# Output products of small experts as full-precision half-array matmuls, in a three-layer kernel on one core

## The chip, the cores and the metric

The kernel runs on one core of a Trainium2 chip. The core has a matrix engine (TensorE, PE in the rows; its weight loads are listed as PEld), a vector engine (VectorE, DVE), a scalar engine (ScalarE, ACT), GpSimd (POOL) and SyncE (SP), which issues most of the transfers. They share one on-chip memory (SBUF) and the accumulators of TensorE (PSUM, eight banks). The metric is the device time of one execution in microseconds (us), the median of several runs.

## The reference

Three layers follow one another: a retention with a decaying state, a dense feed-forward layer, and a routed layer of eight experts.

```
# 1: batch 2, heads 8, 768 steps, head size 64
state = gamma * state + k_t (outer) v_t ;  y_t = scale * q_t @ state
# 2: 1536 tokens, 512 -> 2048 -> 512
h = x @ w_in ;  x = max(0.01 h, h) @ w_out
# 3: each token goes to its best expert e, at most 384 tokens each
e = argmax(x @ w_gate) ;  gate = softmax(x @ w_gate)[e]
out = gate * (max(x @ w1[e], 0) @ w2[e])      # 512 -> 1024 -> 512
```

With the inputs of the reference the router sends 144, 395, 35, 77, 80, 27, 183 and 595 tokens to experts 0 to 7. Of expert 7, 384 are kept, and 128 of these are computed in a pass of their own ahead of the expert loop, so that 256 are left for its body.

## The kernel before

**Precision.** Where a product has to be precise, an operand is split into a high part of reduced precision (`hi`, `gh`) and the rest (`lo`, `gl`), and three one-pass products stand for one: `PROD`, L350, is hi·hi, hi·lo, lo·hi. A plain full-precision (f32) matmul needs no splits; in the trace it shows as two matmul records, each with its own weight load. The split of a weight tile is `conv` (L855): ScalarE writes `hi`, VectorE then writes `lo`.

**The front.** Up to L1040 the program zeroes a tile, runs nine 128x512 matmuls on zeros (L1034), clears one bank (L215) and starts the loads. Then a list written out by hand (`FRONT`, L40) sets the order of the retention and of the first units of the dense layer. After its first entry, the scores `S.0`, stand 22 small matmuls on zeros (L1086). The loop from L1131 on runs the rest of the dense layer; for its first 24 units it also writes three one-element ScalarE instructions each (`tick`, L1155).

**The experts.** `expert(s, cls, o)` (L903) is one expert's body for `cls` tiles of 128 tokens. All three sizes are in the program, and branches on the token count (L1250, L1251) choose one at run time, on each engine by itself. `name_next` (L982) places a hint on the coming branch. A body has eight units `u` of 128 hidden columns. For each, `mm_h` (L825) makes the hidden values, `ew_h` (L876) applies the relu and splits, and `mm_y` (L883) adds the unit to the output bank `yps`. With one tile, `mm_h` takes the f32 weights as they landed (`raw(u)`), four f32 matmuls of 128 columns, and all eight units' hidden values come before the first `mm_y` (`LAGS[1]` is 8). `mm_y` always takes the splits, three matmuls of 512 columns per unit. At unit 6 (one tile) the next expert's rows are transposed (`prep_x`, L779), and the gather of the rows after those is issued.

**Weights.** A unit's weights are one transfer of 512 KB. They land in 15 buffers (`LAND + XLAND`), so that `refill` (L895, issued on SP) of the buffer of unit u loads unit u+15. It waits until u's buffer has been read for the last time. The splits have 8 buffers (`RING + XRING`); `conv_next` (L913) converts the rest of the body's units and the first three of the next body, and may go no further than 8 units past the last `mm_y` (`read`).

**The end of a body.** `evac` (L989) scales the bank by the gate on ScalarE, and `scatter` (L995) writes the rows out with an indirect transfer.

Of the kernel before, what the change touches and what calls it, by code (L numbers as in the profile page):

```python
# [14 lines left out]
ACTF = mybir.ActivationFunctionType  # L15
ALU = mybir.AluOpType
# [43 lines left out]
def retention_moe_moe_kernel(ctx: ExitStack, tc: tile.TileContext, qkv, wb, wc, wg, const, out, cap):  # L60
# [279 lines left out]
    def counts(s):  # L340
        return [r[s // slabs] for r in regs]
# [507 lines left out]
    def raw(u):  # L849
        return craw[slot_of(u, LAND + XLAND)]  # L850
# [21 lines left out]
    def g_of(u, cls):  # L872
        i = u // 4 % 2 if cls == 1 else 0
        return [x[:, i * P:(i + cls) * P] for x in gpair[u % 4]]

    def ew_h(u, cls):  # L876
        hp = h_of(u, cls)
        gh, gl = g_of(u, cls)
        nc.scalar.activation(out=gh, in_=hp, func=ACTF.Relu)  # L879
        nc.vector.scalar_tensor_tensor(out=gl, in0=hp, scalar=0.0, in1=gh.bitcast(F32),  # L880
                                       op0=ALU.max, op1=ALU.subtract)

# [20 lines left out]
    def expert(s, cls, o):  # L903
        u0 = s * PF
        lag = LAGS[cls]
        last = s + 1 == NS
        todo = [(u, cls) for u in range(u0 + (2 if s == 0 else 3), u0 + PF)]
        todo += [(u, 2) for u in range(u0 + PF, min(NU, u0 + PF + 3))]
        filled = [u0]

        read = [u0]

        def conv_next():  # L913
            if todo and todo[0][0] < read[0] + RING + XRING:
                conv(*todo.pop(0))

        def hidden(k):
            u = u0 + k
            r = mm_h(u, cls)
            if u == HOLD or s and k == 0 and cls > 1:  # L920
                held[0] = r
            yield
            ew_h(u, cls)
            conv_next()

        def refills(k):
            if s == 0 and k < HOLD:
                return
            top = todo[0][0] if todo else u0 + PF
            while filled[0] < min(top, u0 + k + 1, u0 + PF):  # L930
                refill(filled[0] + LAND + XLAND)
                filled[0] += 1

        if s == 0:
            finish_all(prep_x(0, cls))
            if NS > 1:
                load_x(1)
            pre_end()
            conv_next()
        xg = None  # L940
        for i in range(lag + PF):
            if i == NAME[cls] and not last:
                name_next(s + 1)
            if i == PREP[cls] and not last:
                xg = prep_x(s + 1)
                step(xg)
                if s + 2 < NS:
                    load_x(s + 2)
            h = hidden(i) if i < PF else None
            if h:  # L950
                step(h)
            k = i - lag
            if k >= 0 and not (last and k >= PF - 2):
                mm_y(u0 + k, cls, range(cls))
                read[0] = u0 + k + 1
            if h:
                step(h)
            else:
                conv_next()
            if i == PREP[cls] and xg is not None:  # L960
                finish_all(xg)
            refills(i)
        while todo:
            conv_next()
        refills(PF)
        for t in range(cls):
            if last:
                for v in (u0 + PF - 2, u0 + PF - 1):
                    mm_y(v, cls, [t])
            evac(s, o, t)  # L970
            scatter(s, o, t)

    def load_counts():
# [15 lines left out]
    def evac(s, o, t):  # L989
        if t == 1:  # L990
            nc.vector.tensor_scalar(out=o[t], in0=yps[t], scalar1=gate(s, t), scalar2=None, op0=ALU.mult)
        else:
            nc.scalar.activation(out=o[t], in_=yps[t], func=ACTF.Copy, scale=gate(s, t))
# [32 lines left out]
    with tc.manual_schedule():  # L1026
# [4 lines left out]
        nc.scalar.activation(out=bias_e, in_=zero[:, 0:1], func=ACTF.Copy)  # L1031
        tick = sm_p.tile([1, 1], F32, name="tick", bufs=1)
        wm = bank("y2", [P, DM])
        for i in range(9):  # L1034
            nc.tensor.matmul(out=wm, lhsT=zb[:, 0:P], rhs=zb[:, 0:DM], start=True, stop=True)
        zero_state(0)
        first_const.append(lambda: load_const(C_D, C_D + 1024))
# [39 lines left out]
        for n in names:  # L1077
            n, c = n.split(".")
            c = [int(x, 16) for x in c]
            if n == "ev" and not rows_l:  # L1080
                early.close()
                rows_p = right.enter_context(tc.tile_pool(name="rows", bufs=1, side="right"))
                rows_l.append(rows_p.tile([P, NT, DM], F32, name="rows"))
            parts[n](*c)
            if n == "S" and c[0] == 0:
                for _ in range(22):  # L1086
                    nc.tensor.matmul(out=wm[0:32, 0:64], lhsT=zb[:, 0:32], rhs=zb[:, 0:64], start=True, stop=True)
            reached += n == "H"
            key = {"S": "q", "qs": "q", "M": "k", "D": "k", "ks": "k"}.get(n)
            if key:  # L1090
                users[key, c[0]].discard(n)
                if not users[key, c[0]]:
                    used((key, c[0]))
# [37 lines left out]
        for i in range(reached, len(units)):  # L1131
# [18 lines left out]
            slot()  # L1150
            if i == len(units) - 1:
                break
            if i - reached < 24:
                for _ in range(3):
                    nc.scalar.activation(out=tick, in_=zero[0:1, 0:1], func=ACTF.Copy)  # L1155
            u = units[i - LAG]
# [169 lines left out]
```

## Time and profile before

| | before |
|---|---|
| median of 3 runs | 524.3 us (523.18, 524.3, 525.4) |
| the profiled execution, its own time | 523.39 us |
| its span, first to last instruction | 521.6 us |
| outside the span | 1.79 us |
| TensorE busy | 506.6 us, 97% of the span |
| VectorE, ScalarE busy | 65%, 49% |
| mean granted TensorE clock | 0.992 |

The busy shares come from one profiled execution. A matmul's duration overlaps the next one's, so that the pace of a row of matmuls is read from the distance between starts. In the trace the bodies of experts 0 to 7 begin on TensorE at 353, 380, 415, 428, 441, 455, 468 and 491 us; experts 2 to 5 take the body for one tile. Where TensorE waits is read from the idle time ahead of its instructions; where its clock falls, from the granted clock of a short stretch.

### The profile page before, as it was taken

Reading aid. Unit: us, or ns where it says so; the run is one execution under the profiler, and the core shown is the slowest. Engines: PE = TensorE matmul, PEld = TensorE weight load, DVE = VectorE, ACT = ScalarE, POOL = GpSimd, SP = SyncE. Lnnn points to the kernel's source line nnn. Section 1 sums busy time; section 2 is a strip of 40 time slices with the busy share of each in tenths; the row PEclk is TensorE's granted clock in tenths of the full one; section 3 lists DMA queues with packets and bytes.
Section 4 is the critical chain, followed back from the end, with each engine's and each line's share of the span. In section 5 each row is a group of like instructions: output and inputs, shape, how many; then the busy total and the mean of one; then the engine's idle time right before and its main releaser. Section 6 shows DMA issues by size and latency. Waiting matters only on the chain.

```text
span 521.6 us, 9204 instructions
## 1 busy us (share of the span) xinstructions
PE 506.6 (97%) x3421; PEld 453.8 (87%) x3421; DVE 337.6 (65%) x666; ACT 253.4 (49%) x573; POOL 49.6 (10%) x79
## 2 busy tenths in 40 slices
PE   7899999999999999999999999999989999999994
PEld 5888989999999999999998888789789899899893
DVE  3999994279779847974732545767544366676550
ACT  2886964365545534442423314346433466666340
POOL 0000000000000000000100106344000121210101
PEclk9999999999999999999999999999989999999998
DMA  8977672022315712220201107589354099992001
GB/s 312 396 261 272 225 252 101 1 81 82 102 31 147 238 50 75 87 80 1 80 1 62 61 1 266 205 283 328 143 198 166 24 369 347 358 351 79 33 1 46
DMA packets 24941, 80.81 MB, mean 155 GB/s; under 512 B 3706, under 2 KB 3834, under 8 KB 24864
## 3 DMA queue, kind: packets, MB, share of 16 engines
q1 hardware_dynamic: 21312, 70.26, 38.6%
q0 software_dynamic: 3552, 9.58, 5.1%
q8 instruction: 41, 0.67, 0.5%
q14 instruction: 36, 0.29, 0.2%
HBM read 72.35 MB, written 9.96 MB: 158 GB/s over the span
## 4 chain that ended last, share of the span: by engine, by line
PE 72%; DMA 22%; DVE 2%; issue 1%; ACT 1%; POOL 0%; SPq 0%; POOLq 0%; ACTq 0%; DVEq 0%
PE ps_h L363 25%; PE ps_y L414 16%; DMA out<-og,gix 12%; PE ps_a L414 7%; DMA xr<-x2d,gix 7%; PE ps_h L837 5%; PE ps_y L889 5%; PE ps_a L190 2%; PE ps_a L256 2%; PE ps_a L245 2%; PE ps_h L715 1%; DMA xpre<-wc,wix 1%; DMA cst<-cst_in 1%; PE ps_y L726 1%; PE ps_h L228 1%
## 5 line engine op out<-in xcount | busy, mean ns | idle before, releaser
L370 ACT ACTIVATE hs<-ps_h 128x384 f32<-128x384 f32 x64 | 31.4, 490 | 95.9 <-PE ps_h L363 95.9
L375 DVE SCALAR_TENSOR_TENSOR hs<-hs 128x384 f32<-128x384 f32 x64 | 35.6, 556 | 65.3 <-ACT hs L370 65.1
L414 PE MATMUL ps_y<-hi,gh 128*128 128x512 f32 x138 | 56.4, 409 | 0.0
L363 PE MATMUL ps_h<-xh,hi 128*128 128x384 f32 x256 | 56.3, 341 | 0.0
L363 PE MATMUL ps_h<-xl,hi 128*128 128x384 f32 x256 | 55.5, 338 | 0.0
L363 PE MATMUL ps_h<-xh,lo 128*128 128x384 f32 x256 | 55.5, 338 | 0.0
L379 ACT ACTIVATE gh<-hs 128x384 fp32r<-128x384 f32 x64 | 33.7, 526 | 43.8 <-DVE hs L375 43.8
L414 PE MATMUL ps_y<-hi,gl 128*128 128x512 f32 x138 | 53.9, 391 | 0.0
L414 PE MATMUL ps_y<-lo,gh 128*128 128x512 f32 x138 | 53.8, 390 | 0.0
L363 PEld LDWEIGHTS ps_h<-xh,hi 128*128 128x128 f32 x256 | 45.9, 188 | 4.8
L385 DVE TENSOR_TENSOR gl<-hs,gh 128x384 fp32r<-128x384 f32 x64 | 35.6, 557 | 21.3 <-ACT gh L379 21.3
L363 PEld LDWEIGHTS ps_h<-xl,hi 128*128 128x128 f32 x256 | 45.9, 187 | 0.0
L363 PEld LDWEIGHTS ps_h<-xh,lo 128*128 128x128 f32 x256 | 45.8, 187 | 0.0
L889 PE MATMUL ps_y<-hi,gh 128*128 128x512 f32 x104 | 41.1, 395 | 0.0
L889 PE MATMUL ps_y<-hi,gl 128*128 128x512 f32 x104 | 40.8, 392 | 0.0
L889 PE MATMUL ps_y<-lo,gh 128*128 128x512 f32 x104 | 40.8, 392 | 0.0
L860 DVE TENSOR_TENSOR lo<-xland,hi 128x1024 fp32r<-128x1024 f32 (+1 forms) x32 | 33.5, 1056 | 7.2 <-ACT hi L859 7.1
L880 DVE SCALAR_TENSOR_TENSOR gl<-ps_h,gh 128x256 fp32r<-128x256 f32 (+2 forms) x42 | 16.6, 395 | 33.1 <-ACT gh L879 30.4
L879 ACT ACTIVATE gh<-ps_h 128x256 fp32r<-128x256 f32 (+2 forms) x42 | 15.3, 364 | 39.6 <-PE ps_h L837 22.9
L860 DVE TENSOR_TENSOR lo<-land,hi 128x1024 fp32r<-128x1024 f32 (+1 forms) x30 | 30.9, 1042 | 5.4 <-ACT hi L859 5.4
L414 PEld LDWEIGHTS ps_y<-hi,gl 128*128 128x128 f32 x138 | 25.9, 188 | 5.6
L414 PEld LDWEIGHTS ps_y<-hi,gh 128*128 128x128 f32 x138 | 25.9, 187 | 4.3 <-issue 0.3
(201 smaller groups left out, 998.1 us busy)
## 6 DMA issues: line engine op xcount, KB each, us to landing
land<-wc SPq DMA_DIRECT2D x32, 512.0 KB, 6.6
xland<-wc SPq DMA_DIRECT2D x32, 512.0 KB, 5.9
land<-wb SPq DMA_DIRECT2D x31, 512.0 KB, 4.9
land<-qkv SPq DMA_DIRECT2D x19, 512.0 KB, 5.3
out<-zero SPq DMA_DIRECT2D x12, 256.0 KB, 5.7
x2d<-rows SPq DMA_DIRECT2D x12, 256.0 KB, 2.2
early<-qkv SPq DMA_DIRECT2D x5, 512.0 KB, 7.4
cst<-cst_in SPq DMA_DIRECT2D x1, 512.0 KB, 5.5
```

Of the source, the lines that this page charges most:

```text
L190: nc.tensor.matmul(out=at["s", c][h2][:, a, :], lhsT=kT[r, a, :], rhs=qT[r, a, :], start=True, stop=True)
L363: nc.tensor.matmul(out=h_ps, lhsT=w[i][:, dc * P:(dc + 1) * P], rhs=x[j][:, dc, :], start=(n == 0), stop=(n == 3 * KD - 1))
L370: nc.scalar.activation(out=hs, in_=gt[u][0], func=ACTF.Copy)
L375: nc.vector.scalar_tensor_tensor(out=hs, in0=hs, scalar=0.01, in1=hs, op0=ALU.mult, op1=ALU.max)
L379: nc.scalar.activation(out=gh, in_=gt[u][0], func=ACTF.Copy)
L385: nc.vector.tensor_tensor(out=gl, in0=hs, in1=gh.bitcast(F32), op=ALU.subtract)
L414: nc.tensor.matmul(out=yb[ti][t], lhsT=gt[u][i][:, t * P:(t + 1) * P], rhs=w[j][:, 512:1024], start=(f == fs[0] and n == 0), stop=(f == fs ...
L837: r = nc.tensor.matmul(out=hp, lhsT=w[i][:, dc * P:(dc + 1) * P], rhs=(h, l)[j][:, dc, 0:cls * P], start=(n == 0), stop=(n == 3 * KD - 1))
L860: nc.vector.tensor_tensor(out=lo[:, o], in0=src[:, o], in1=hi[:, o].bitcast(F32), op=ALU.subtract)
L879: nc.scalar.activation(out=gh, in_=hp, func=ACTF.Relu)
L880: nc.vector.scalar_tensor_tensor(out=gl, in0=hp, scalar=0.0, in1=gh.bitcast(F32), op0=ALU.max, op1=ALU.subtract)
L889: nc.tensor.matmul(out=yps[t], lhsT=gg[i][:, t * P:(t + 1) * P], rhs=w[j][:, 512:1024], start=(k == 0 and n == 0), stop=(k == PF - 1 and n ...
```

## The change

- **`ew_h`:** with one tile, ScalarE also writes an f32 copy of the relu of the first 64 tokens (`g_half`, 64 columns per unit, in the no longer needed mask part of `cst`).
- **`y_group` in place of `mm_y`, one-tile bodies only:** the output products stand in two groups of four units, each with a branch on TensorE. With at most 64 tokens a unit is one f32 matmul of 64 by 512, straight on `raw(u)`; even units write partitions 0 to 63 of the bank, odd units 64 to 127. Otherwise the group is the old split products.
- **`join`:** with at most 64 tokens, ScalarE copies the upper half of the bank to SBUF and VectorE adds it, times the gate, to the output rows. Both have a branch of their own.
- **`refills`:** in one-tile bodies a buffer may be refilled only after its `y_group` (`read`), since that group may read it.
- **The start:** 27 small and 5 wide matmuls on zeros instead of 9 wide ones; the 22 small ones after `S.0` go; the `tick` instructions stop after 11 units, not 24.

The conversions of all weights stay, also those that a body with at most 64 tokens does not read.

```diff
+    def g_half(u):
+        return cst[:, C_D + u % PF * 64:C_D + u % PF * 64 + 64]
+    def few(s, cls):
+        return (s % slabs) * BW + cls * P - 64
+    def y_group(s, cls, ks):
+        us = [s * PF + k for k in ks]
+        t = cls - 1
+        with tc.If(counts(s)[0] <= few(s, cls)) as c:
+            for u in us:
+                k = u % PF
+                nc.tensor.matmul(out=yps[t][k % 2 * 64:k % 2 * 64 + 64, :], lhsT=g_half(u), rhs=raw(u)[:, 512:1024],
+                                 start=(k < 2), stop=(k >= PF - 2), skip_group_check=True)
+        with c.Else():
+            for u in us:
+                mm_y(u, cls, [t])
+    def join(s, cls, o):
+        part = cst[0:64, C_D + 512:C_D + 1024]
+        with tc.If(counts(s)[1] <= few(s, cls)):
+            nc.scalar.activation(out=part, in_=yps[cls - 1][64:P, :], func=ACTF.Copy)
+        with tc.If(counts(s)[2] <= few(s, cls)):
+            nc.vector.scalar_tensor_tensor(out=o[0:64, :], in0=part, scalar=gate(s, cls - 1)[0:64, :],
+                                           in1=o[0:64, :], op0=ALU.mult, op1=ALU.add)
 def ew_h(u, cls):
         nc.scalar.activation(out=gh, in_=hp, func=ACTF.Relu)
+        if cls == 1:
+            nc.scalar.activation(out=g_half(u), in_=hp[:, 0:64], func=ACTF.Relu)
 def expert(s, cls, o):
-            while filled[0] < min(top, u0 + k + 1, u0 + PF):
+            while filled[0] < min(top, u0 + k + 1, u0 + PF, read[0] if cls == 1 else NU):
...
-            if k >= 0 and not (last and k >= PF - 2):
+            if cls > 1 and k >= 0 and not (last and k >= PF - 2):
                 mm_y(u0 + k, cls, range(cls))
                 read[0] = u0 + k + 1
+            if cls == 1 and k in (0, 4):
+                end = PF - 2 if last and k else k + 4
+                y_group(s, cls, range(k, end))
+                read[0] = u0 + end
...
             evac(s, o, t)
+            if cls == 1:
+                join(s, cls, o[t])
             scatter(s, o, t)
 the start
-        for i in range(9):
+        for i in range(27):
+            nc.tensor.matmul(out=wm[0:32, 0:64], lhsT=zb[:, 0:32], rhs=zb[:, 0:64], start=True, stop=True)
+        for i in range(5):
             nc.tensor.matmul(out=wm, lhsT=zb[:, 0:P], rhs=zb[:, 0:DM], start=True, stop=True)
...
-            if n == "S" and c[0] == 0:
-                for _ in range(22):
-                    nc.tensor.matmul(out=wm[0:32, 0:64], lhsT=zb[:, 0:32], rhs=zb[:, 0:64], start=True, stop=True)
...
-            if i - reached < 24:
+            if i - reached < 11:
                 for _ in range(3):
                     nc.scalar.activation(out=tick, in_=zero[0:1, 0:1], func=ACTF.Copy)
```

The order of the instructions, at three places. First TensorE in the one-tile body of expert 2, where the hidden products (L831) end and the output products begin (before):

```order
L831 MATMUL ps_y<-cxf,xland 128x128 x5
L758 UNCONDITIONAL_BRANCH x2
L831 MATMUL ps_y<-cxf,xland 128x128 x3
L889 MATMUL ps_y<-hi,gh 128x512
L889 MATMUL ps_y<-lo,gh 128x512
L889 MATMUL ps_y<-hi,gl 128x512
```

The same place on TensorE after the change; L888 is the f32 form (`land` is a weight buffer, `cst` holds `g_half`), L917 the split form:

```order
L831 MATMUL ps_y<-cxf,xland 128x128 x2
L885 COMPARE_AND_BRANCH
L888 MATMUL ps_y<-land,cst 64x512 x4
L885 UNCONDITIONAL_BRANCH
L917 MATMUL ps_y<-hi,gh 128x512
L917 MATMUL ps_y<-lo,gh 128x512
L917 MATMUL ps_y<-hi,gl 128x512
```

A branch now chooses between four f32 matmuls and the twelve split ones of four units; a second such piece follows for the other four. Second, TensorE at the end of that body, where the program goes on to the choice of the next body (before):

```order
L889 MATMUL ps_y<-hi,gh 128x512
L889 MATMUL ps_y<-lo,gh 128x512
L889 MATMUL ps_y<-hi,gl 128x512
L1250 UNCONDITIONAL_BRANCH
L1250 COMPARE_AND_BRANCH
L1251 COMPARE_AND_BRANCH
L837 MATMUL ps_h<-cxh,hi 128x256 x4
```

The same place after the change (L1287 and L1288 are the former L1250 and L1251):

```order
L917 MATMUL ps_y<-hi,gl 128x512
L885 UNCONDITIONAL_BRANCH
L896 UNCONDITIONAL_BRANCH
L898 UNCONDITIONAL_BRANCH
L1287 UNCONDITIONAL_BRANCH
L1287 COMPARE_AND_BRANCH
L1288 COMPARE_AND_BRANCH
L837 MATMUL ps_h<-cxh,hi 128x256 x4
```

Three block ends stand ahead of the old branches. Third, ScalarE at the end of expert 5's one-tile body: the conversions of the next body's first three units (L859), the evacuation (L993), and the first relu of the two-tile body that follows (before):

```order
L859 ACTIVATE hi<-land 128x1024
L758 UNCONDITIONAL_BRANCH
L859 ACTIVATE hi<-land 128x1024 x2
L993 ACTIVATE og<-ps_y,tab 128x512
L1250 UNCONDITIONAL_BRANCH
L1250 COMPARE_AND_BRANCH
L1251 COMPARE_AND_BRANCH
L879 ACTIVATE gh<-ps_h 128x256
L859 ACTIVATE hi<-land 128x1024
```

The same place after the change (L1031 is the evacuation, L897 the copy of `join`, L905 the relu):

```order
L859 ACTIVATE hi<-land 128x1024 x3
L885 UNCONDITIONAL_BRANCH
L1031 ACTIVATE og<-ps_y,tab 128x512
L896 COMPARE_AND_BRANCH
L897 ACTIVATE cst<-ps_y 64x512
L896 UNCONDITIONAL_BRANCH x2
L898 UNCONDITIONAL_BRANCH
L1287 UNCONDITIONAL_BRANCH
L1287 COMPARE_AND_BRANCH
L1288 COMPARE_AND_BRANCH
L905 ACTIVATE gh<-ps_h 128x256
L859 ACTIVATE hi<-land 128x1024
```

The three conversions now stand behind the first group of output products, and the copy of `join` and its branch stand between the evacuation and the next body's relu.

## Rows read from the trace of the kernel before

**Rows 1.** The page, part 1: the span; then TensorE's waits in total.

```profile
span 521.6 us, 9204 instructions
...
PE ps_h L837 <- issue: 3.5, 2, 2.7
```

**Rows 2.** Stretch; busy PE, PEld, DVE, ACT, POOL; clock; DMA; GB/s: experts 2, 6.

```profile
415.00:428.10 13.10, 13.10 (x93) 12.11 (x93) 8.96 (x18) 8.73 (x18) 3.83 (x4) 1.00 0.90 328
468.20:491.20 23.00, 23.00 (x153) 20.77 (x152) 13.95 (x19) 12.69 (x20) 1.03 (x1) 1.00 0.20 67
```

**Rows 3.** Timeline of PE (start, duration): output products of experts 2, 5; next body.

```profile
422.52 0.48 PE L889 MATMUL ps_y<-hi,gh 128*128 128x512 f32 x1
...
428.13 1.95 PE L831 MATMUL ps_h<-cxf,xland 128*128 128x128 f32 x16
...
462.63 0.48 PE L889 MATMUL ps_y<-hi,gh 128*128 128x512 f32 x1
...
468.21 0.63 PE L837 MATMUL ps_h<-cxh,hi 128*128 128x256 f32 x4
```

**Rows 4.** Chain of waits in the front: f32 matmuls, whole array and half.

```profile
23.13 0.89 PE ps_a L245 x8
24.02 1.02 PE ps_a L256 x16
```

**Rows 5.** Line 256: its weight loads (count, ns min/median/max, first and last start).

```profile
L256 PEld LDWEIGHTS ps_a<-am,land x160: 132/137/138, 18.0 to 76.3; 128*64 128x64 f32 x160
```

**Rows 6.** Branches on TensorE (ns, first and last start): choice of body; near branch.

```profile
L1250 PEldq COMPARE_BRANCH  x1: 2211/2211/2211, 424.0 to 424.0; - x1
...
L1250 PEldq COMPARE_BRANCH  x1: 3399/3399/3399, 437.1 to 437.1; - x1
...
L1250 PEldq COMPARE_BRANCH  x1: 4229/4229/4229, 450.2 to 450.2; - x1
...
L758 PEldq COMPARE_BRANCH  x8: 77/226/242, 359.1 to 474.1; - x8
```

**Rows 7.** TensorE at the start of expert 1 (timeline), and the granted clock behind.

```profile
379.61 0.94 PE L837 MATMUL ps_h<-cxh,hi 128*128 128x384 f32 x4 [2.66 <-issue]
...
381.90:382.90 1.00, 1.00 (x5) 1.00 (x4) 0.00 (x0) 0.00 (x0) 0.00 (x0) 0.50 0.00 0
```

**Rows 8.** Timelines of ACT, DVE and PE where expert 6 follows expert 5.

```profile
463.61 2.96 ACT L859 ACTIVATE hi<-land 128x1024 fp32r<-128x1024 f32 x3
...
468.40 0.69 ACT L993 ACTIVATE og<-ps_y,tab 128x512 f32<-128x512 f32 x1 [1.84 <-PE ps_y L889]
...
464.99 3.48 DVE L860 TENSOR_TENSOR lo<-land,hi 128x1024 fp32r<-128x1024 f32 x3
...
472.76 1.22 DVE L860 TENSOR_TENSOR lo<-xland,hi 128x1024 fp32r<-128x1024 f32 x1
...
474.12 0.65 PE L837 MATMUL ps_h<-cxh,lo 128*128 128x256 f32 x4
```

**Rows 9.** SP's timeline: refills in expert 2's body; DMA in one stretch.

```profile
416.15 4.75 SPq L897 DMA_DIRECT2D land<-wc  x6
...
423.00:425.00 2.00, 2.00 (x10) 1.60 (x10) 1.02 (x3) 1.70 (x4) 0.00 (x0) 1.00 1.03 414
```

**Rows 10.** Timeline of the start, on PE and DVE.

```profile
1.17 4.02 PE L1035 MATMUL ps_y<-zero 128*128 128x512 bf16 x9 [1.17 <-DVE zero L1030]
...
5.38 1.16 PE L190 MATMUL ps_a<-early 64*128 64x128 f32 x16
6.47 0.81 PE L1087 MATMUL ps_y<-zero 128*32 128x64 bf16 x22
8.13 1.10 PE L256 MATMUL ps_a<-am,early 128*64 128x128 f32 x16 [0.84 <-DVE am L212]
...
6.80 1.29 DVE L212 TENSOR_TENSOR am<-ps_a,cst 128x512 f32<-128x512 f32 x2 [5.68 <-DMA cst<-cst_in]
```

**Rows 11.** Line 1155: count, ns min/median/max, first and last start.

```profile
L1155 ACT ACTIVATE tick<-zero x72: 184/202/204, 101.5 to 197.6; 1x1 f32<-1x1 f32 x72
```

More of the change, by code (lines that the diff above doesn't have):

```diff
@@ L962, in expert @@
             refills(i)
+        if last:
+            read[0] = u0 + PF
         while todo:
@@ L966, in expert @@
         for t in range(cls):
-            if last:
+            if last and cls == 1:
+                y_group(s, cls, (PF - 2, PF - 1))
+            elif last:
                 for v in (u0 + PF - 2, u0 + PF - 1):
```

## Prediction

> **What bounds the kernel now.** I read the page's first part and the sum of TensorE's waits first: of 521.6 us TensorE is busy for 97%, and its largest wait in all is 3.5 us, in two pieces, ahead of hidden products of the expert bodies [rows 1]. So work taken off TensorE is time gained, where the others keep up. The chain of waits names transfers for the last fifth; I don't follow it there, since the busy time by stretch shows TensorE busy for 13.10 of 13.10 us in expert 2's body and 23.00 of 23.00 in expert 6's, with ScalarE and VectorE at two thirds or less [rows 2]. The change bears on the bodies of experts 2 to 5, and of these only 2 (35 tokens) and 5 (27 tokens) take the half-array form; 3 and 4 (77 and 80) keep the split products inside a branch. The second thing to see is what stands close behind TensorE at the end of such a body: the branch to the next body [rows 6] and the weight splits of the next three units [rows 8].
>
> **The output products.** Before, they take 24 one-pass matmuls, from 422.52 to 428.13, which is 5.61 us, and from 462.63 to 468.21, which is 5.58 [rows 3]. After, they are 8 f32 matmuls, 16 records. The pace of such records is in the front of the kernel: on the whole array 8 records of 128 columns take 0.89 us, 0.111 each; on alternating halves 16 records take 1.02 us, 0.064 each [rows 4]. So the halves overlap, though not fully. The two records of one matmul share a half and follow each other, only the second can run beside the next matmul's first, and 16 records take 9 places in a row: 9 x 0.111 = 1.00, nearly the 1.02 seen. With 512 columns a place is four times as long, 0.445, and nine are 4.0 us. Gain: 5.6 - 4.0 = 1.6 us per body, **3.2 us** in two. Bounds: 8 places, 3.6 us per body, so 4.0 gained; and one place lost between the two groups, 4.4 per body, so 2.4 gained.
>
> [...] The rows show 160 weight loads of 64 columns, 137 ns each, in those half-array rows [rows 5], and 16 of them fit beside 16 matmuls in 1.02 us, at 64 ns a piece: they are hidden. [...]
>
> **The branches on TensorE.** Two groups mean two more branches per one-tile body. A near branch took 0.077 to 0.242 us [rows 6]. The sequencer passes it while matmuls are queued: free in itself. It matters where the sequencer is late already, at the choice of the next body. That branch began at 424.0 in expert 2, 1.5 us after the output products began, and took 2.21 us; in the next two bodies it took 3.40 and 4.23 us [rows 6]. Before, it had 5.6 - 1.5 = 4.1 us of queued matmuls as cover. With the half-array form the body ends 4.0 us after the output products begin, so the cover is 2.5 us. From expert 2 to 3 the branch jumps far, and I take 3.3, about the mean of the three: a gap of **0.8 us** (0 at 2.2, 1.7 at 4.2). The other half-array body, expert 5, goes on to the two-tile body next in the program. For expert 4's exit, where 4.23 us already exceed the cover by 0.1, the three block ends and a near branch add **0.2 us** (0 to 0.4).
>
> [...]
>
> **The splits ahead of expert 6.** This body has two tiles and needs splits at once. Before, in its 23.00 us TensorE waits nowhere, but barely: the split of its fifth unit ends at 472.76 + 1.22 = 473.98, and the matmul that needs it starts at 474.12 [rows 8]. The chain to it begins with the first three conversions on ScalarE at 463.61, as soon as the first unit of output products is done [rows 8]. After, they wait for the whole first group, 462.63 + 2.2 = 464.8, and end at 467.8; then the evacuation (0.69), the new copy (half the partitions, the same 512 columns; I take 0.7 with its branch), the relu (0.4) and the conversion (1.05): near 470.8. On VectorE the three splits, 3.48 us as a block, end at 469.5, then the join (0.7), `gl` (0.4) and the fourth split (1.2) end near 472.1, the fifth near 473.5. TensorE, which starts the body 1.6 us earlier, would want the fourth at 471.2 and the fifth at 472.6. It waits **1.0 us** in all (0, if the engines overlap better; 1.6, when all of expert 5's gain is lost).
>
> **What is free.** The extra relu is 8 ScalarE instructions per one-tile body, at most 0.3 us each by the nearest row (0.38 for 128x256 [rows 8] is a bound): ScalarE has 13.10 - 8.73 = 4.4 us to spare in such a body [rows 2], 2.8 once it is 1.6 shorter, for 2.4; its cover is gone only at expert 6, counted above. In experts 3 and 4 the split products are the same in number. The `tick` instructions are 72 of 0.2 us between 101 and 198 us [rows 11]; TensorE has no wait there to give back, so taking 39 away gives nothing.
>
> **The refills** move on SP from each unit's hidden products to after its group. In expert 2's body the first stood at 416.15 [rows 9]; now the first four follow the first group, at 422.52 + 2.2 = 424.7. SP has nothing else to do behind them. The transfer engines reach 414 GB/s [rows 9], 1.3 us per 512 KB, so four take about 5 us and land by 431. The first of them is the last unit of expert 3, wanted for its split near 433: cover of about 2 us. Later ones have more, since expert 3's refills load expert 5's units. Cost 0, and up to 1 us if they land later.
>
> **The start.** S.0 starts at 5.38 and ends at 6.47, and the masks behind it start at 6.80 because of a transfer [rows 10]. [...] Between S.0 and the products at 8.13, 22 small matmuls go, and the gap becomes 1.6 us. Cost 0, if the clock does as before; if not, a rival.
>
> **The sum.** -3.2 + 0.8 + 0.2 + 1.0 = -1.2 us. Against the profiled execution's own 523.39: 522.2. The three runs' median is 0.9 above that execution, so -1.2 on the median would be 523.1. I put the forecast halfway, **522.7**; this case alone spans 520.8 (2.6 gained from 523.39) to 524.6 (no gain by the median, with a little run scatter).
>
> **Rivals.**
> - **The full gain arrives.** The far branch takes 2.2 us, as it did in this very place before, and expert 6's splits keep up: -3.2 + 0.2 = -3.0, **520.9** against the midpoint of 523.9. For it: that 2.21. Against: 3.40 and 4.23 for the same branch in its neighbours, and splits that had 0.14 us to spare.
> - **Slower: the halves don't overlap at 512 columns.** Sixteen records one behind the other take 16 x 0.445 = 7.1 us, 1.5 more per body, +3.0 in two; the two waits don't arise then, the 0.2 stays: **527.1**. It decides from a pace of 0.35 us per record (5.6 / 16). Against it stand the half-array rows, which overlap with two operand streams as well.
> - **The weight loads don't hide.** The matmuls overlap, and 16 loads of 0.137 us [rows 5] add 2.2 us to each body: -1.2 + 4.4 - 1.8, since the two waits don't arise, is +1.4, **525.3**. Against it: those loads are hidden behind matmuls a quarter as long. [...]
> - **The clock at the start.** Small matmuls use a quarter of the columns, and the idle gap after S.0 doubles. A gap of 2.66 us at expert 1 was followed by a granted clock of 0.50 [rows 7]; 1.6 us is shorter. If TensorE runs the first two f32 stretches at half the clock, S.0 (1.1) and the products at 8.13 (1.1) double: +1.1 (part of S.0's hides under the transfer) to +2.2, and more if it goes on; with the sum, **524.4**.
> [...]
>
> **How the numbers follow.** About 0.5%, 2.6 us, is what a measurement of this kernel can tell from no change. Forecast 0.48 (within 0.5% but for its edge, 0.03 faster); full gain 0.20 (faster); no overlap 0.07 (slower); weight loads 0.02 (within); start 0.10 (0.07 within, 0.03 slower); moved code 0.13 (0.05 faster, 0.03 within, 0.05 slower). Faster 0.28, within 0.57, slower 0.15. The range runs from 520.0, just below the full gain, to 525.4, past the start's case; outside are no overlap and most of the moved code.
>
> **What the profile after would show.** The 16 records of experts 2 and 5 at about 0.25 us apart, 4.0 us in all (7 would mean no overlap); a gap on TensorE at the start of expert 3 with the body branch beside it; a wait of expert 6's first products for VectorE's splits; no wait for a landing weight in experts 3 and 4; a granted clock of 1.00 and S.0 at 0.07 us a record in the first 10 us. I am wrong if the output products take over 4.5 us, if the waits exceed the gain, or if the stall at expert 1 changes by more than 1 us.

## The result, and the profile after

The changed kernel takes 528.01 us (median of 13 runs, 524.88 to 529.73), the kernel before 524.1 in the same series (13 runs, 521.12 to 525.91): a ratio of 1.0075, 95% interval 1.0057 to 1.0094. It is slower, by about 3.9 us, where the forecast was 522.7 us and the range ended at 525.4. The profiled execution of the changed kernel took 528.01 us itself, with a span of 526.2, beside 521.6 before [rows 1].

The page of the changed kernel, its span, and TensorE's busy time (busy us, share of the span, instructions):

```profile
span 526.2 us, 9227 instructions
...
PE 504.1 (96%) x3404; PEld 449.3 (85%) x3406; DVE 338.4 (64%) x668; ACT 249.7 (47%) x568; POOL 51.3 (10%) x79
```

TensorE's waits in the changed kernel (us in total, times, longest):

```profile
PE ps_h L837 <- issue: 6.7, 2, 4.7
...
PE ps_y L831 <- DVE og L899: 0.6, 1, 0.6
```

The first line is the one to see: the two pieces that were 3.5 us before [rows 1] are 6.7 now. "issue" is time in which the engine waited for nothing that the profile shows. The second line is a wait that did not exist before.

A table by stretch, from the first TensorE row of each body to that of the next, in us. So a gap ahead of a body counts in the stretch before it. The three columns on the right are experiments told below. Each column is one execution; that of the last is the fastest of its 12 (518.94 us, median 520.97).

| stretch | before | change | new in 2 to 5 | code moved | moved, join on GpSimd |
|---|---|---|---|---|---|
| up to expert 0 | 352.99 | 355.18 | 354.80 | 353.44 | 353.47 |
| expert 0 | 26.62 | 28.65 | 26.70 | 26.90 | 26.72 |
| expert 1 | 35.41 | 36.65 | 33.90 | 35.44 | 33.83 |
| expert 2 | 13.11 | 11.96 | 12.09 | 12.35 | 11.94 |
| expert 3 | 13.11 | 14.25 | 14.24 | 14.24 | 13.56 |
| experts 4, 5 | 26.97 | 24.78 | 24.78 | 24.78 | 24.77 |
| experts 6, 7 | 46.54 | 48.04 | 45.67 | 45.72 | 46.56 |
| TensorE's last end | 514.75 | 519.51 | 512.18 | 512.87 | 510.85 |

Experts 2, 4 and 5 are faster, by 3.3 us in all. Everything else is slower, and most of it in places whose executed instructions the change doesn't touch: experts 0, 1, 6 and 7 have two or three tiles.

The output products of expert 2, then of expert 5 up to the next body, in TensorE's timeline (start, duration) of the changed kernel:

```profile
428.86 2.79 PE L888 MATMUL ps_y<-land,cst 128*64 128x512 f32 x12
431.48 1.03 PE L888 MATMUL ps_y<-xland,cst 128*64 128x512 f32 x4
432.44 2.19 PE L831 MATMUL ps_h<-cxf,xland 128*128 128x128 f32 x16
...
467.88 2.36 PE L888 MATMUL ps_y<-xland,cst 128*64 128x512 f32 x9
...
470.08 0.59 PE L888 MATMUL ps_y<-xland,cst 128*64 128x512 f32 x1
470.09 1.45 PE L888 MATMUL ps_y<-land,cst 128*64 128x512 f32 x5
...
471.47 0.74 PE L837 MATMUL ps_h<-cxh,hi 128*128 128x256 f32 x4
```

They take 432.44 - 428.86 = 3.58 us and 471.47 - 467.88 = 3.59, where rows 3 have 5.61 and 5.58. That is 2.0 us gained in each. The rows at 470.08 and 470.09, of two buffers, show how: a record of one half starts together with a record of the other. The loss, then, is elsewhere. The start of expert 1 in the timeline, the granted clock behind it (stretch; length, busy time of PE, PEld, DVE, ACT and POOL; clock; DMA share; GB/s), and the two jumps ahead of it (count, ns min/median/max, first and last start):

```profile
383.83 1.62 PE L837 MATMUL ps_h<-cxh,hi 128*128 128x384 f32 x4 [4.68 <-issue]
...
384.50:388.50 4.00, 4.00 (x14) 4.00 (x14) 0.00 (x0) 0.31 (x1) 0.00 (x0) 0.50 0.00 0
...
L1288 PEldq COMPARE_BRANCH  x2: 3334/4274/5215, 374.8 to 378.5; - x2
```

Rows 7 had a gap of 2.66 us here. Now it is 4.68, since one of the two jumps takes 5.2 us. TensorE, idle in the gap, comes back at a granted clock of 0.50 and stays there until about 390 (0.50 from 388.5 to 390 us, 0.98 from 390 to 391): expert 1 takes 36.65 us, where an execution that keeps its clock takes 33.9. A second such place is expert 7, whose body follows expert 6's by a jump and stops after three matmuls:

```profile
494.81 0.51 PE L837 MATMUL ps_h<-cxh,hi 128*128 128x256 f32 x3
497.32 0.28 PE L837 MATMUL ps_h<-cxh,hi 128*128 128x256 f32 x1 [2.00 <-issue]
```

Before, this gap was 0.83 us:

```profile
494.27 0.62 PE L837 MATMUL ps_h<-cxh,lo 128*128 128x256 f32 x3 [0.83 <-issue]
```

And there is the wait in expert 3, for its third unit of hidden products; TensorE's row, and VectorE's row of the join:

```profile
435.26 0.94 PE L831 MATMUL ps_y<-cxf,xland 128*128 128x128 f32 x6 [0.63 <-DVE og L899]
...
434.47 0.73 DVE L899 SCALAR_TENSOR_TENSOR og<-cst,tab,og 64x512 f32<-64x512 f32 x1
```

### The profile page after: what moved, and what is told of

It reads as the page before. It is cut to its first block, busy times and chain, and to the rows that moved or that the text cites. A ratio compares the mean times of both kernels' runs of the same rounds, so it can differ in the third digit from the quotient of the medians.

```text
span 526.2 us, 9227 instructions
## 1 busy us (share of the span) xinstructions
PE 504.1 (96%) x3404; PEld 449.3 (85%) x3406; DVE 338.4 (64%) x668; ACT 249.7 (47%) x568; POOL 51.3 (10%) x79
## 4 chain that ended last, share of the span: by engine, by line
PE 71%; DMA 20%; DVE 3%; issue 3%; ACT 1%; POOL 0%; POOLq 0%; SPq 0%; DVEq 0%; ACTq 0%
PE ps_h L363 25%; PE ps_y L414 16%; DMA out<-og,gix 9%; DMA xr<-x2d,gix 8%; PE ps_a L414 7%; PE ps_h L837 5%; PE ps_y L917 5%; PE ps_a L256 2%; PE ps_a L190 2%; PE ps_a L245 2%; DMA xpre<-wc,wix 2%; DMA cst<-cst_in 1%; PE ps_h L228 1%; PE ps_a L464 1%; PE ps_a L450 1%
## 5 line engine op out<-in xcount | busy, mean ns | idle before, releaser
L414 PE MATMUL ps_y<-hi,gh 128*128 128x512 f32 x138 | 56.4, 409 | 0.0
L414 PE MATMUL ps_y<-hi,gl 128*128 128x512 f32 x138 | 53.9, 391 | 0.0
L414 PE MATMUL ps_y<-lo,gh 128*128 128x512 f32 x138 | 53.8, 390 | 0.0
L905 ACT ACTIVATE gh<-ps_h 128x256 fp32r<-128x256 f32 (+2 forms) x42 | 15.6, 371 | 44.8 <-PE ps_h L837 27.3
L917 PE MATMUL ps_y<-hi,gh 128*128 128x512 f32 x88 | 34.6, 394 | 0.0
L917 PE MATMUL ps_y<-hi,gl 128*128 128x512 f32 x88 | 34.5, 392 | 0.0
L917 PE MATMUL ps_y<-lo,gh 128*128 128x512 f32 x88 | 34.5, 392 | 0.0
L859 ACT ACTIVATE hi<-xland 128x1024 fp32r<-128x1024 f32 (+1 forms) x32 | 29.4, 930 | 0.7 <-PE ps_y L888 0.5
```

Of the source, the lines that this page charges most:

```text
L414: nc.tensor.matmul(out=yb[ti][t], lhsT=gt[u][i][:, t * P:(t + 1) * P], rhs=w[j][:, 512:1024], start=(f == fs[0] and n == 0), stop=(f == fs ...
L859: nc.scalar.activation(out=hi[:, o], in_=src[:, o], func=ACTF.Copy)
L917: nc.tensor.matmul(out=yps[t], lhsT=gg[i][:, t * P:(t + 1) * P], rhs=w[j][:, 512:1024], start=(k == 0 and n == 0), stop=(k == PF - 1 and n ...
```

## The experiments

**The theory** is that the change lost its time by the place of code, not by executed work. Every one-tile body grew by some 40 instructions of TensorE code, also those that are never executed, so that all bodies behind expert 0's lie elsewhere. The rivals are the new start, the executed branches and the join. Lengths of code are counted in the compiled kernel, an f32 matmul as four instructions and a tiny bf16 one as two.

### The start alone, and the change without it

The kernel before with the new start (27 tiny and 5 wide zero matmuls, none behind S.0, `tick` bound 11):

> The kernel before with the changed start alone (27 tiny and 5 wide zero matmuls, no 22 behind S.0, ticks 11); expert bodies as before, two instructions of TensorE code more ahead of them. If the new start costs the 1 to 2 us that the front, the offsets and the pre-stage had lost by the profile after, this run is 525.3 to 526.3 us beside 524.1. If the loss sits in the expert bodies, it is 524.1 within 0.5, with the first row of expert 1 on TensorE 2.7 us behind the row before it, as before.

Measured: 523.98 us, ratio 1.0017 (1.0004 to 1.0029). The change with the old start:

> The change with the start of before (9 wide zero matmuls, 22 tiny ones behind S.0, ticks 24); all of the new expert bodies. If the bodies carry the loss: 528 within 0.7, the gap ahead of expert 1 near 4.7 us and the one in expert 7 near 2.0 us. If the start carries it: 525.5 to 527.

Measured: 526.23 us, ratio 1.0051 (1.0034 to 1.0067), with gaps of 4.84 and 2.31 us ahead of expert 1 and in expert 7. The second's gaps are about those expected if the bodies carry the loss; its time lies in the range named for the start. Against the change the ratio is lower by 0.24%, 1.3 us, and the two intervals overlap; the first run alone gives 0.9 us. So the start costs about 1 us, but it neither makes the gaps nor the larger part of the loss.

The traces show where most of this 1 us goes: into expert 2, where the start changes nothing that is executed. ScalarE's first relu of that body, before and with the new start alone, then ScalarE's branch into the body and TensorE's third pair of units, both with the new start alone:

```profile
416.26 0.28 ACT L879 ACTIVATE gh<-ps_h 128x128 fp32r<-128x128 f32 x1 [0.35 <-PE ps_h L831]
...
418.99 0.28 ACT L879 ACTIVATE gh<-ps_h 128x128 fp32r<-128x128 f32 x1 [2.55 <-PE ps_y L831]
...
L1249 ACTq COMPARE_BRANCH  x1: 65/65/65, 416.3 to 416.3; - x1
...
419.72 2.20 PE L831 MATMUL ps_h<-cxf,land 128*128 128x128 f32 x16 [0.43 <-DVE gl L880]
```

With the new start ScalarE begins 2.6 us after its branch (0.6 before), VectorE follows late, and TensorE waits for VectorE: the body takes 13.96 us in place of 13.11, and with the new bodies 11.96 in the change in place of 11.29 with the old start. All 13 profiles with the new start show this relu 2.1 to 4.0 us behind the body's start on TensorE, all three with the old start 1.2. On ScalarE the new start is 39 `tick` instructions fewer. So here, too, a move of code, ScalarE's this time, fits; no run tests it by itself.

### The new bodies only where they are executed

```diff
+    NEW = (2, 3, 4, 5)
...
-            if cls == 1:
+            if cls == 1 and s in NEW:
                 join(s, cls, o[t])
```

(and the like at each of the change's places in `expert` and `ew_h`; elsewhere the old one-tile body)

> The whole change, but the one-tile bodies of experts 0, 1, 6 and 7, which are never executed, have the form of before, so that the code ahead of expert 1's bodies is two instructions longer than before in place of 43, and ahead of expert 7's 180 in place of 313. Every executed instruction is that of the change. Theory of the code's positions: the gap ahead of expert 1 is 2.7 us again (4.7 in the change), the low clock behind it is short again, and the time is 2 to 4 us under the change's 528.0. Rival, that the executed work itself (start, branches, join) costs the 3.9 us: 528.0 within 0.7, gap 4.7.

Measured: **520.85 us**, ratio 0.9955 (0.9935 to 0.9974): faster than the kernel before, and 7.2 us under the change by the medians (6.3 by the ratios, each against the kernel before in its own series), with the same executed instructions. The start of expert 1, and the clock behind it:

```profile
381.50 0.94 PE L837 MATMUL ps_h<-cxh,hi 128*128 128x384 f32 x4 [2.41 <-issue]
...
384.50:388.50 4.00, 4.00 (x24) 3.92 (x23) 3.21 (x4) 2.64 (x4) 0.00 (x0) 1.00 0.89 293
```

The gap is back at 2.41, and in this execution the clock is not lost behind it. By the table, the change's profile is behind this one by 2.0 us in expert 0, 2.8 in expert 1, 2.4 in experts 6 and 7, and 0.4 ahead of expert 0; experts 2 to 5 agree within 0.2, and TensorE ends 7.3 us later. The theory holds; the rival that executed work costs the time has fallen.

### The kernel before, with dead code

```diff
+    def dead(n, o):
+        for _ in range(n):
+            nc.tensor.matmul(out=o[0:32, 0:64], lhsT=zb[:, 0:32], rhs=zb[:, 0:64], start=True, stop=True)
...
+            if k == 0 and cls == (3 if s in (2, 3, 4, 5) else 1):
+                dead(20, yps[0])
```

> The kernel before with 20 tiny zero matmuls on TensorE in each expert's bodies that are never executed (the one-tile body of experts 0, 1, 6, 7; the three-tile body of experts 2 to 5), some 40 instructions of code per expert and no executed work. Theory of the code's positions: the gap ahead of expert 1 grows from 2.7 to near 4.7 us and the one in expert 7 from 0.8 to 2.0 us, and the time is 2 to 4 us over 524.1. Rival, that positions do nothing: 524.1 within 0.5 and the gaps as before.

Measured: 526.67 us, ratio 1.0064 (1.0041 to 1.0087). Nothing more is executed, and 3.3 us are lost. The start of expert 1, and the jumps ahead of it:

```profile
383.07 1.26 PE L837 MATMUL ps_h<-cxh,hi 128*128 128x384 f32 x4 [4.34 <-issue]
...
L1257 PEldq COMPARE_BRANCH  x2: 3734/4138/4543, 374.4 to 378.4; - x2
```

The gap came as expected. The one in expert 7 did not: it is gone here, and two others of 0.51 and 0.47 us stand inside experts 3 and 4. So 40 instructions per body alone don't say where the gaps come up.

### Place or length

All bodies grown to about 256 instructions, by 107 tiny matmuls in those never executed:

> The whole change, and 107 tiny zero matmuls more on TensorE in bodies that are never executed (the one-tile body of experts 0, 1, 6, 7; the three-tile body of 2 to 5), so that the TensorE code of each expert is about 256 instructions longer than before in place of 42: later than before, but at about the same place within stretches of 256 instructions. Executed work is that of the change. If the place within such a stretch decides: the gap ahead of expert 1 is 2.4 to 2.7 us, the one in expert 7 under 0.9, and the time 521 to 523 us. If the length of code that is jumped over decides: the gap ahead of expert 1 is 4.7 us or more, and the time 528 or more.

Measured: 534.65 us, ratio 1.0214 (1.0175 to 1.0254). Each theory got half. TensorE's waits of the kind "issue":

```profile
PE ps_h L831 <- issue: 5.4, 2, 2.8
PE ps_y L831 <- issue: 4.0, 1, 4.0
PE ps_h L837 <- issue: 2.7, 1, 2.7
```

The last line is the gap ahead of expert 1, 2.72 us and short again, and expert 7 has none: there the place decides. The first two lines are new: 2.6 us ahead of expert 2, and 2.8 and 4.0 us inside experts 4 and 5, 10 and 23 matmuls behind the first, as expert 7's gap in the change came three matmuls behind. All three follow a jump past the two-tile and the three-tile body, now 214 instructions longer, to the one-tile body. The code there lies at about the same place within stretches of 256 instructions as before, so the longer jump, or what goes with it, may be what costs here; but expert 3 is reached by the same kind of jump and has no gap. The granted clock falls as well: by the page it is 0.7 and 0.8 in the slices from 440 and from 467 us, which hold the ends of the gaps in experts 4 and 5, and 0.9 or more in the slices beside them. These two bodies take 36.76 us, where the change takes 24.78. That 256 instructions are the length that counts was the author's assumption and is not shown: in the table below the gap is short at 200 (2.97 us) and at 254 (2.91 and 2.76) too.

To separate the two at expert 1, dead code went into expert 0's one-tile body alone, ahead of everything else that moves, in the kernel with the new bodies in 2 to 5:

```diff
+            if k == 0 and s == 0 and cls == 1:
+                dead(20, yps[0])      # 20, 60 or 100 tiny matmuls
```

> The kernel with the new one-tile bodies in experts 2 to 5 alone (520.85 us), with 20 tiny zero matmuls in the one-tile body of expert 0 alone, which is never executed: some 42 instructions of TensorE code more ahead of expert 1, as in the change. If the place of expert 1's code alone makes the long gap: 4.3 to 4.8 us ahead of expert 1 (2.4 without), the low clock behind it, and 524 to 525.5 us. If the growth of all bodies is needed: gap 2.4 to 2.7, 520.9 us.

> As the kernel with 20 tiny matmuls in expert 0's one-tile body, with 60, some 123 instructions. One look, for the gap ahead of expert 1. If the gap grows with the length of the code jumped over: over 5 us. If it goes by the place within a stretch of 256 instructions: it can lie anywhere between 2.4 and 5 us, and need not be longer than with 20.

> As the kernel with 20 tiny matmuls in expert 0's one-tile body, with 100, some 198 instructions. One look, for the gap ahead of expert 1. Length: longer than with 60. Place: nearer to the 2.4 to 2.7 us that an added 0 and an added 254 instructions gave than with 20.

Measured: 524.16 us with 20 (ratio 1.0015, 0.9994 to 1.0035), 3.3 us over the same kernel without; its gap, 4.02 us, is a little under the expected 4.3 to 4.8. A single execution gave 525.14 with 60, another 519.99 with 100. All profiles, by the code ahead of expert 1 (instructions more than in the kernel before; the longer of the two jumps; the gap; the clock granted from 381 to 391 us):

| kernel | more code | jump, us | gap, us | clock |
|---|---|---|---|---|
| before | 0 | 3.47 | 2.66 | 0.85 |
| start alone | 2 | 3.39 | 2.49 | 1.00 |
| new in 2 to 5 | 2 | 3.31 | 2.41 | 1.00 |
| never half (below) | 2 | 3.52 | 3.05 | 0.66 |
| join without branch (below) | 2 | 3.62 | 2.63 | 0.83 |
| join on GpSimd (below) | 2 | 3.62 | 3.21 | 0.83 |
| second hint (below) | 8 | 3.63 | 2.59 | 0.83 |
| old start | 41 | 4.96 | 4.84 | 0.66 |
| dead code | 42 | 4.54 | 4.34 | 0.83 |
| change | 43 | 5.22 | 4.68 | 0.66 |
| 20 in expert 0 | 44 | 4.70 | 4.02 | 0.83 |
| 60 in expert 0 | 125 | 4.96 | 4.65 | 0.66 |
| 100 in expert 0 | 200 | 3.57 | 2.97 | 1.00 |
| code moved (below) | 254 | 3.57 | 2.91 | 0.85 |
| moved, join on GpSimd (below) | 254 | 3.44 | 2.76 | 1.00 |
| all padded | 256 | 3.74 | 2.72 | 1.00 |

The longer jump takes 3.3 to 3.7 us with 0 to 8 and with 200 to 256 instructions more, and 4.5 to 5.2 with 41 to 125. It neither grows with the length nor follows what is executed: ahead of expert 1 the place decides. What makes the two kinds of place is not settled by these runs.

### The half-array form, the join, a hint

In the kernel with the new bodies in 2 to 5, the bound in `few` set to -1, so that the same code takes the old products:

> The kernel with the new one-tile bodies in experts 2 to 5 alone (520.85 us), in which the bound that the branches compare with is -1 for every expert: the same code at the same places, every branch executed, but the products of experts 2 and 5 go the old way, and there is no copy and no join. By the pieces in the traces (output products 5.6 in place of 3.6 us, twice; the wait of expert 3 for the join, 0.63 us, gone): 520.85 + 4.0 - 0.6 = 524.2 us. By the prediction's step for expert 6, which would lose 1.0 us of the gain there, 523.2. If the half form gains nothing in the end: 520.9.

Measured: 524.27 us, ratio 1.0009 (0.9987 to 1.0032), 3.4 us over the kernel with the form by the medians, as the pieces said, but 2.8 by the ratios. Not all of it need be the form: this profile has a lost clock behind expert 1's gap and the other has not. From the start of expert 2 to that of expert 6, which leaves this out, the form gains 53.72 - 51.11 = 2.6 us: 1.9 in expert 2 and 1.8 in expert 5, less 1.1 in expert 3, where the pieces had only the wait of 0.6.

The copy and the join without their branches:

```diff
-        with tc.If(counts(s)[1] <= few(s, cls)):
+        if s in (2, 5):
...
-        with tc.If(counts(s)[2] <= few(s, cls)):
```

> The kernel with the new one-tile bodies in experts 2 to 5 alone (520.85 us), with the copy and the join without their branches: always in experts 2 and 5, not at all in 3 and 4. The same instructions are executed, but for the branches of ScalarE and VectorE. If TensorE's wait for the join in expert 3 (0.63 us) comes from the branch, behind which a wait for an earlier instruction of VectorE turns into one for the join: the wait is gone, 520.2 us. If it is the join's own data: the wait stays, 520.9 us.

Measured: 522.57 us, ratio 0.9981 (0.9962 to 1.0), over both expected times; expert 1 lost its clock in this profile. The wait for the join stays at 0.63 us: it is not the branch. So the join itself was taken off VectorE:

```diff
-        with tc.If(counts(s)[2] <= few(s, cls)):
-            nc.vector.scalar_tensor_tensor(out=o[0:64, :], in0=part, scalar=gate(s, cls - 1)[0:64, :],
-                                           in1=o[0:64, :], op0=ALU.mult, op1=ALU.add)
+        with tc.If(counts(s)[3] <= few(s, cls)):
+            nc.gpsimd.tensor_scalar(out=part, in0=part, scalar1=gate(s, cls - 1)[0:64, :], scalar2=None, op0=ALU.mult)
+            nc.gpsimd.tensor_tensor(out=o[0:64, :], in0=part, in1=o[0:64, :], op=ALU.add)
```

> The kernel with the new one-tile bodies in experts 2 to 5 alone (520.85 us), with the join on GpSimd (a multiplication and an addition, behind a branch of its own) in place of VectorE. In expert 3 TensorE's third unit of hidden products waits 0.63 us for the join, also where the join has no branch. Theory: its PSUM bank, free since the middle of expert 2, is waited for as the end of VectorE's whole body, because the bank has other users in the bodies of two and three tiles; then the wait is gone without the join on VectorE, expert 3 takes 13.1 to 13.5 us in place of 14.24, and the time is 520.0 us. Rival: the wait is for data that the join's neighbours make (the copy on ScalarE, the turned rows): it stays, 520.9 us, under another name.

Measured: 521.75 us, ratio 0.9958 (0.9936 to 0.9979). TensorE in expert 3, where the second row's `ps_y` is the third unit's bank, and the weight loads of that row:

```profile
429.17 2.05 PE L831 MATMUL ps_h<-cxf,xland 128*128 128x128 f32 x16
431.33 2.05 PE L831 MATMUL ps_y<-cxf,xland 128*128 128x128 f32 x16
...
431.33 1.86 PEld L831 LDWEIGHTS ps_y<-cxf,xland 128*128 128x128 f32 x16 [0.30 <-DVE lo L860]
```

The wait for the join is gone and expert 3 takes 13.56 us in place of 14.24. The remaining 0.4 us over the 13.11 of before stand between these two rows: 2.16 us from start to start, where before it is 1.79 (428.13 to 429.92). The weight loads wait there for VectorE's `lo`, which is now the last of expert 2's body. So in both kernels TensorE waits for the last of VectorE's queue in expert 2: for the join 0.63 us, for `lo` 0.30. That the cause is the bank's use in other bodies fits, but was only argued.

The time is over both expectations, and the ratio is that of the kernel with the join on VectorE (0.9955). What expert 3 gains goes again at expert 6. One `lo` there takes 1.99 us, where the others take 1.2, next to the join on GpSimd, and TensorE waits for it:

```profile
472.21 1.99 DVE L860 TENSOR_TENSOR lo<-xland,hi 128x1024 fp32r<-128x1024 f32 x1
...
474.25 0.74 PE L837 MATMUL ps_h<-cxh,lo 128*128 128x256 f32 x4 [0.34 <-DVE lo L860]
```

Experts 6 and 7 take 46.31 us here, and 45.67 with the join on VectorE.

The gap ahead of expert 1 itself, by a second branch hint:

```diff
+            tc.mark_branch_hint_location(f"two{s}", hint=under(s, e, 2), engines=[e])
```

> The kernel with the new one-tile bodies in experts 2 to 5 alone (520.85 us), with a second branch hint for each expert, for the branch between the two-tile and the three-tile body, besides the one for the choice of one tile. It adds 6 instructions of code per expert. If the gap ahead of expert 1 (2.4 us, a jump to the three-tile body without a hint) is the wait for that code: the gap falls under 1 us, and the time is 518.5 to 519.5 us. If only one hint counts, or a later one takes the place of the first: gap as before or another far jump late, 520.9 us or more.

Measured: 528.48 us, ratio 1.0107 (1.0075 to 1.0138). The gap stays at 2.59, and other places wait: 1.09 us of "issue" ahead of expert 2, 0.71 and 0.47 ahead of transposes, and 1.00, 0.97 and 1.76 us for VectorE and ScalarE, which come late. So the second hint does not add to the first; the rival holds.

### The whole change, moved

All new bodies, and 106 tiny matmuls in expert 0's one-tile body:

> The whole change with all of its new bodies, and 106 tiny zero matmuls in the one-tile body of expert 0 alone, which is never executed: all TensorE code from expert 1 on lies 213 instructions later, so that expert 1's stands 254 behind before's in place of 43. If the place of the code is what the change lost by: the gap ahead of expert 1 is 2.4 to 3.2 us (4.7), the one in expert 7 under 0.9 (2.0), and the time 521 to 523 us in place of 528.0. If it was something else that also left with the old bodies in experts 0, 1, 6 and 7: 527 to 529, whatever the gap ahead of expert 1. If the length of the code counts: 529 or more.

Measured: **521.51 us**, ratio 0.9970 (0.9954 to 0.9986). The same with the join on GpSimd:

> The same, with the join on GpSimd in place of VectorE. By the wait in expert 3 (0.63 us, and 1.1 us of that body): 0.5 to 1.0 us under the kernel with the moved code alone. If the scatter of the gap ahead of expert 1 is larger than this: within 0.7 of it.

Measured: **520.97 us**, ratio 0.9954 (0.9935 to 0.9973). Expert 1 in the first of the two, and the clock:

```profile
380.34 1.45 PE L837 MATMUL ps_h<-cxh,hi 128*128 128x384 f32 x4 [2.91 <-issue]
...
384.50:388.50 4.00, 4.00 (x24) 4.00 (x23) 2.85 (x4) 2.78 (x4) 0.00 (x0) 1.00 0.78 204
...
490.00:496.00 6.00, 6.00 (x52) 1.00 0.19 69
```

The gap ahead of expert 1 is 2.91 us, the one in expert 7 is gone (the last row, of TensorE alone, is busy throughout), and the whole change with one piece of dead code is faster than before. Between ratios 1.0075 and 0.9970 lie 1.05%, or 5.5 us (about 4 to 7, by the two intervals): that much of the change's time goes by the place of its code. The 0.5 us that the join on GpSimd gains in the medians is as large as expected, but inside the scatter, and the profiles don't show it: by the table it gains 0.7 us in expert 3 and loses 0.8 in experts 6 and 7.

## Why the prediction was wrong

- **The output products: right in kind, under-sized.** Nine places, 4.0 us, were taken as the value, eight (3.6) as the bound. The 16 records took 3.58 and 3.59, which is eight places of 0.45 us: the halves overlap fully, and the gain is 4.0 us, not 3.2. The step "only the second can run beside the next matmul's first" was wrong. It came from durations in the chain of waits, which include what overlaps the next row. By the distance between starts the 16 records of rows 4 take 24.88 - 23.95 = 0.93 us in the kernel before, nearer to eight places of 0.111 (0.89) than to nine (1.00):

```profile
23.95 1.09 PE L256 MATMUL ps_a<-am,land 128*64 128x128 f32 x16
24.88 0.63 PE L228 MATMUL ps_h<-land,ks 128*64 128x64 f32 x16
```

- **The weight loads: right.** The trace has the 32 loads of 128x64, 18 from `land` and 14 from `xland`; their median is 137 ns, as in rows 5, and they add nothing to the eight places.

```profile
L888 PEld LDWEIGHTS ps_y<-land,cst x18: 132/137/137, 428.9 to 470.5; 128*64 128x64 f32 x18
...
L888 PEld LDWEIGHTS ps_y<-xland,cst x14: 133/137/137, 431.1 to 469.7; 128*64 128x64 f32 x14
```

- **The far branch out of expert 2: wrong.** 0.8 us was the mean of three branches of rows 6. It took 0.44 us, and no gap came:

```profile
L1287 PEldq COMPARE_BRANCH  x1: 439/439/439, 429.8 to 429.8; - x1
```

  The three of rows 6 were taken as a price of that branch. They were prices of one state of the code: in the kernel before with dead code, which executes the same instructions, the same three branches take 1.31, 0.43 and 0.67 us where rows 6 have 2.21, 3.40 and 4.23. This is the same error as below, here in the kernel's favour. Place is not all of it: in the two runs that differ in the bound alone (-1 or not), with the code in the same places, they differ by 0.6 to 1.1 us.
- **Expert 4's exit: 0.2 lost was said, 0.3 gained.** Expert 4 takes 13.08 us where it took 13.38; its branch takes 1.14 us in place of 4.23.
- **The splits ahead of expert 6: over-sized.** 1.0 us was summed. In the change the profile lists no wait for them, and expert 6 reaches its first output product 0.3 us later than before (7.17 us after its start, 6.85 before). ScalarE and VectorE nearly caught up, close to the lower bound of 0.
- **What is free: the join was not.** VectorE's spare time in a body was weighed, and expert 6, but not who waits for VectorE's end in expert 3. That cost 0.63 us as a wait, and 1.1 in the body. The extra relu took 0.23 us (median), under its bound of 0.3; the row of 0.38 us that the prediction quotes from rows 8 is not among its lines, but the trace has it, at 469.91.
- **The start: 0 was said, about 1 us was measured**, by two comparisons of runs. Most of it, 0.7 to 0.9 us, is in expert 2, where ScalarE arrives late; the prediction looked for the cost in the front alone. TensorE's arrival at expert 0 scatters: 353.0 to 354.8 us in the three profiles with the old start, 353.1 to 355.2 in the 13 with the new. The rival of the clock at the start came in one of these 13, the new bodies in 2 to 5: a granted clock of 0.51 from 8 to 10 us, where the products take 2.00 us instead of 1.10.
- **The code moves: the step that failed.** Moved code (all bodies behind expert 0's lie elsewhere) had a chance of 0.13, mostly outside the range, and the sum had it at nothing. Between two places of the same code it measured +5.5 us. At the other place the change is 0.30% faster than before (0.14 to 0.46), 1.6 us, beside the sum's 1.2. That these are close is luck: of the sum's errors, four in favour of the kernel (0.8, 0.8, 0.5 and 0.7 us) and two against it (1.1 and about 1.0) largely cancel, and the gap of 0.83 us in expert 7, which the kernel before has, is gone at the other place as well. What the change is worth apart from any place stays open.

More could have been read from the rows. The far jumps of rows 6 take 2.2 to 4.2 us, a spread of 2 us for the same line in neighbouring bodies: a sign that the price of such a jump is not fixed. And the two signs of moved code, given 0.05 each, are not alike: TensorE's waits of the kind "issue" ahead of hidden products were 3.5 us in all [rows 1], so shorter jumps can give back no more than this and the clock behind it, while for longer ones no row sets an end.

## What to carry to other kernels

This program has a price that no instruction shows, by where the code of its large bodies lies: the same executed instructions took 520.85 and 528.01 us. Before an added branch or body is judged by its time, put the same number of instructions into a body that is never executed; if the kernel alone moves by as much, the comparison is of places. Here one such filler turned 0.75% slower into 0.3% faster, with nothing executed changed. And of an engine with time to spare, ask who waits for the end of its queue, and whether it still arrives in time when its own code moves.

## What the runs showed of the hardware

- The longer of TensorE's two jumps ahead of expert 1 takes 3.3 to 3.7 or 4.5 to 5.2 us by the place of the code (16 profiles), and some 40 instructions per expert that are never executed cost 3.3 us in a kernel of 524.
- The clock behind a gap is not a matter of the gap's length alone: with gaps of 2.41, 2.49, 2.72, 2.76 and 2.97 us ahead of expert 1 the granted clock from 381 to 391 us was 1.00, while with 2.59, 2.63, 2.66, 2.91, 3.05, 3.21 and all from 4.0 on it was 0.66 to 0.85. Expert 1 takes 33.8 to 34.0 us in the first kind and 35.4 to 36.7 in the second, "issue" waits at its end taken off. This fits the scatter of some 4 us between executions of one kernel: of the 12 of the moved code with the join on GpSimd, the four with a mean granted clock of 0.997 or more take 518.9 to 520.2 us, the two with 0.989 take 523.1 and 523.2.
- The matmuls of 512 f32 columns on the two column halves ran fully side by side here, weight loads included: 16 records in 3.58 us, 0.45 a pair. One record at a time takes 0.445 by estimate, four times the 0.111 of rows 4.
- In both profiles with the join on GpSimd, a VectorE `tensor_tensor` on 128x1024 that begins while GpSimd's `tensor_tensor` on 64x512 runs takes 1.99 us in place of 1.2.
